# Block 0's attention scores in eight visits instead of nine, with the last head group spread over eight later visits

## The chip, the core and the metric

The kernel runs on one core of a Trainium2 chip. The metric is the device time of one execution in microseconds (us). The engines of the core run side by side, each through its own list of instructions in order: TensorE (PE in the profile, its weight loads PEld), VectorE (DVE), ScalarE (ACT), GpSimd (POOL) and SyncE (SP, which here only starts DMAs). They wait for each other by semaphores.

## The reference

A transformer layer on 2048 tokens of width 1024: attention over a sliding window of 256 with 32 heads of width 32, then a dense part of width 3584. Inputs are bf16.

```python
qkv = layernorm(x) @ wqkv                     # 32 heads of 32
scores = einsum("bhqd,bhkd->bhqk", q, k) * 32 ** -0.5
mask = (i - j >= 0) & (i - j < 256)
p = softmax(where(mask, scores, -1e9))
h = x + einsum("bhqk,bhkd->bhqd", p, v) @ wo
h2 = h + silu(layernorm(h) @ w1) @ w2
```

## The kernel before

The 2048 tokens are four **blocks** of 512 (`b`), and the 32 heads eight **groups** of four (`g`). The pair has one number, `i = 8 * b + g`; `G` is 8.

*The dense stream.* PE computes V, then Q and K by block, then the output projection `wo`, in groups of eight matmuls of 512 columns (`v_group`, `qk_group`, `wo_group`). A group accumulates in one of three PSUM banks in turn (`next_acc`; banks 0 to 2 of `four`), and then a copy, here on DVE, takes it to SBUF (`CAST` at L262 or L272). After this come the two matmuls of the dense part (L786, L814), which the change does not touch.

*Attention in the stream.* `between(kt)` is called ahead of each dense matmul and counts them; a count is called a **slot** below (the first matmul of Q and K of block 0 is slot 0). At fixed slots it runs one of two things:

- a **visit** computes scores. The scores are transposed (keys on partitions, 64 at a time; queries along the columns), and one matmul uses 32 rows by 64 columns of PE, so that the four heads of a group and the two halves of 64 keys run side by side. A visit computes one **unit** of all four heads into `sc` (four banks, one for each head), and up to three extra heads of other units, each 512 columns, into single banks;
- a **piece** (`attn_piece`) multiplies the masked exponentials of two heads of one group with V (18 matmuls in block 0, 24 later) into bank 3, and DVE normalises the result from there (`attn_norm`: a reciprocal at L482, a multiplication at L483) into one of three `obuf` buffers. After the second piece of a group a transposing DMA (L491) takes it from `obuf` to `qT`, whose columns are no longer needed as queries.

*The three extra banks of a visit.* When a visit runs, `now` is the bank that the dense group is filling. `idle` is the next one, which the next group will fill; `behind` is the one that the previous group filled, free once DVE has copied it; `out` is bank 3, free once the last piece's norm has read it:

```python
now = acc_n[0] % 3
idle, behind, out = (now + 1) % 3, (now + 2) % 3, 3
```

Every visit starts after four matmuls of a dense group. After its scores, ACT exponentiates each extra bank and then `sc` (`exp_c`, `exp_0`, `exp_xy`; L328, L428, L334 and L335), and POOL zeroes what the window's edges cut off (`select`, L461).

*Block 0* has 16 units (`2 * g` and `2 * g + 1`). The first nine visits (`visit_0`, slots 108, 132, 148 and so on to 244) compute one unit and three heads of others each, as `VISITS_0` lists: 63 of the 64 heads. The 64th, head 3 of unit 15, is computed in the first visit of period 0.

*Blocks 1 to 3* go in twelve **periods** (`p`) of 48 slots, from slot `t = 256 + 48 * p`, two groups (`i`, `i + 1`) in each. A period has three visits, at `t + 4`, `t + 20` and `t + 36` (`visit(i, n)`, n = 0, 1, 2), and four pieces, at `t + 42`, `t + 47`, `t + 59` and `t + 76`; the last two fall into the next period. The units X and Y of a group and its edge blocks C are shared out over the visits. n = 1 and n = 2 have three extra heads (one C in `idle`, two of X in `out` and `behind`); n = 0 has two (two of C in `idle` and `out`), and in period 0 a third, head 3 of unit 15, in `behind`.

*The order inside a visit* is made in `scores`, L375 to L397. For each head and half it lists the extra bank's matmuls and those of `sc`: banks in `ahead` (`idle`, and `out` in n = 0) go before `sc`, others behind. Each matmul gets a position `at`, the number of columns of its head that come before it, and L388 sorts by that:

```python
todo.sort(key=lambda m: m[0])
```

*Storage.* Block 0's exponentials lie in `r_e`, five columns of 128 for each head, at the offsets of `POS_0`. `r_a` holds queries, keys and V; `qT[3]` and `kT[3]` in it are filled by `qk_group` in block 3 (slots 512 to 703).

Of the kernel before, what the change touches and what calls it, by code (L numbers as in the profile page):

```python
# [11 lines left out]
ACT = mybir.ActivationFunctionType  # L12
ALU = mybir.AluOpType

P = 128
# [22 lines left out]
    [(0, "X", 2), (1, "Y", 1), (2, "X", 3)],  # L38
    [(1, "Y", 2), (2, "C", 1), (3, "Y", 3)],
]  # L40
POS_0 = [(0, 3072, 5632, 7936, 8192, 10752)["ZABNCD".index(c)] for c in "ZCABCDZBACDBZAND"]
VISITS_0 = [
# [3 lines left out]
]  # L46
PIECE_0 = {"X": (0, 128, 512, 320), "Y": (0, 128, 256, 512)}
FIRST = [
# [6 lines left out]
def kernel(  # L55
# [49 lines left out]
    def view(region, off, *dims):  # L105
        n = 1
        for d in dims:
            n *= d
        ap = region[:, off:off + n]
        if len(dims) == 2:  # L110
            return ap.rearrange("p (a b) -> p a b", b=dims[1])
        if len(dims) == 3:
            return ap.rearrange("p (a b c) -> p a b c", b=dims[1], c=dims[2])
        return ap
# [29 lines left out]
    def full_of(e):  # L144
        return e[:, 2048:2560].rearrange("p (h q) -> p h q", q=P)

    obuf = [view(r_n, 512 * i, 4, P) for i in range(3)]
    h_blk = [view(r_a, w2_off + 4096 * 4, 4, D)] + [view(r_e, 8192, 4, D)] * 3
    ln2T = [view(r_a, w2_off + 4096 * 5, KT, 512), view(r_e, 0, KT, 512), view(r_e, 4096, KT, 512), view(r_e, 0, KT, 512)]

# [152 lines left out]
    def chunk_of(i, bank, piece, h):  # L303
        if i >= G and bank == "C":
            return c_ring[:, (i + 1) % 3, h, piece * P:(piece + 1) * P]
        if i >= G:
            c0 = 2048 + mid_at(i, bank, h) * P if piece == 2 else h * 512 + (piece - piece // 3) * P
        else:
            c0 = POS_0[2 * i + (bank != "X")] + h * 640 + (384 if bank == "C" else PIECE_0[bank][piece])
            return r_e[:, c0:c0 + P]  # L310
        return (xbuf if bank == "X" else ybuf)(i)[:, c0:c0 + P]

    def unit_xy(i, odd):
        q0 = odd * P
        mid, first, last = odd, odd - 2, odd + 2
        return [
            [(i, mid, q0, q0 + 320, 64), (i, last, q0 + 256, q0 + 384, 384), (i, first, q0, q0 + 64, 0)],
            [(i, mid, q0 + 64, q0 + 384, 128), (i, first, q0, q0 + 128, 0), (i, last, q0 + 320, q0 + 384, 448)],
        ]

    def unit_c(i):
        pair = (i, i + 1) if (i + 1) % 3 < (i + 2) % 3 else (i + 1, i)
        return [[(ii, kt, q * P, q * P + P, (n * 2 + m) * P)
                 for n, ii in enumerate(pair) for m, (kt, q) in enumerate(((-1, 0), (2, 3)))]] * 2
# [17 lines left out]
    def visit(i, n):  # L342


        now = acc_n[0] % 3
        idle, behind, out = (now + 1) % 3, (now + 2) % 3, 3
        if n == 0:
            own, e_own = unit_xy(i, 0), xbuf(i)
            more = [(1, idle, unit_c(i)), (2, out, unit_c(i))]
            if i == G:  # L350
                more.append((3, behind, unit_0(15)))
        elif n == 1:
            own, e_own = unit_xy(i, 1), ybuf(i)
            more = [(3, idle, unit_c(i)), (0, out, unit_xy(i + 1, 0)), (1, behind, unit_xy(i + 1, 0))]
        else:
            own, e_own = unit_xy(i + 1, 1), ybuf(i + 1)
            more = [(0, idle, unit_c(i)), (2, out, unit_xy(i + 1, 0)), (3, behind, unit_xy(i + 1, 0))]
        scores(own, more, (idle, out)[:2 if n == 0 else 1])
        side = [h for h, _, unit in more if n and len(unit[0]) == 3]
        for h, bank, unit in more:  # L360
            if h in side:
                exp_xy(xbuf(i + 1), four[bank].rearrange("p (h q) -> p h q", h=1), h, h + 1, mid_at(i + 1, "X", h))
            elif len(unit[0]) == 4:
                exp_c(i, h, bank)
            else:
                exp_0(15, h, bank)
                select_0(15, h, h + 1)
                join_0(15, h, h + 1)
        if side:
            select_xy(xbuf(i + 1), side[0] // 2)  # L370
        exp_xy(e_own, sc[:], 0, 4)
        for pair in range(2):
            select_xy(e_own, pair)

    def scores(own, more, ahead):  # L375
        todo = []
        for h in range(4):
            for half in range(2):
                runs = [(sc[:, h, :], own[half])]
                for hh, bank, unit in more:  # L380
                    if hh == h:
                        runs.insert(0 if bank in ahead else 1, (four[bank], unit[half]))
                at = 0
                for bank, parts in runs:
                    for p in parts:
                        todo.append((at, h, half, bank, p))
                        at += p[3] - p[2]
        todo.sort(key=lambda m: m[0])  # L388
        for _, h, half, bank, (ii, kt, qa, qb, col) in todo:
            b, g = divmod(ii, G)  # L390
            t = b * 4 + kt
            r0, k0 = h * DH, (t % 4) * P + half * 64
            nc.tensor.matmul(  # L393
                bank[half * 64:half * 64 + 64, col:col + qb - qa],
                lhsT=kT[t // 4][r0:r0 + DH, g, k0:k0 + 64], rhs=qT[b][r0:r0 + DH, g, qa:qb],
                start=True, stop=True, tile_position=(r0, half * 64),
            )  # L397

    def unit_0(m):
        i, odd = divmod(m, 2)  # L400
        if odd:
            return [
                [(i, 1, 128, 448, 0), (i, 3, 384, 512, 320), (i, 2, 448, 512, 448)],
                [(i, 1, 128, 512, 0), (i, 3, 448, 512, 384), (i, 2, 448, 512, 448)],
            ]
        return [[(i, 0, 0, 320, 0), (i, 2, 256, 448, 320)], [(i, 0, 0, 384, 0), (i, 2, 320, 448, 384)]]

    def heads_0(m, h0, h1):
        return r_e[:, POS_0[m] + 640 * h0:POS_0[m] + 640 * h1].rearrange("p (h q) -> p h q", q=640)

    def select_0(m, h0, h1):
        e = heads_0(m, h0, h1)

        if m % 2:
            select(e[:, :, 0:P], e[:, :, 0:P], True)
            select(e[:, :, 512:640], e[:, :, 320:448], True)
            select(e[:, :, 256:384], e[:, :, 256:384], False)
        else:
            select(e[:, :, 512:640], e[:, :, 256:384], False)
            select(e[:, :, 0:P], e[:, :, 0:P], True)  # L420
            select(e[:, :, 320:448], e[:, :, 320:448], True)
# [2 lines left out]
        nc.gpsimd.tensor_copy(out=heads_0(m, h0, h1)[:, :, 384:448], in_=heads_0(m - 1, h0, h1)[:, :, 448:512])  # L424

    def exp_0(m, h, bank):
        at = POS_0[m] + 640 * h
        nc.scalar.activation(out=r_e[:, at:at + 512], in_=four[bank], func=ACT.Exp, scale=scale)  # L428

    def visit_0(k):  # L430

# [48 lines left out]
    def attn_norm(i, pair):  # L480
        recip = small.tile([P, 8, 1], F32, name="recip", tag="recip")
        nc.vector.reciprocal(out=recip[:], in_=o_ps[:, :, DH:VW])  # L482
        nc.vector.tensor_tensor(  # L483
            out=obuf[i % 3][:, :, pair * 64:(pair + 1) * 64].rearrange("p t (h d) -> p t h d", d=DH),
            in0=o_ps[:, :, 0:DH].rearrange("p (t h) d -> p t h d", h=2),
            in1=recip[:].rearrange("p (t h) o -> p t h o", h=2).to_broadcast([P, 4, 2, DH]), op=ALU.mult,
        )

    def attn_transpose(b, g):
        i = b * G + g  # L490
        nc.sync.dma_start_transpose(out=qT[b][:, g, :].rearrange("p (t q) -> p t q", q=P),  # L491
                                    in_=obuf[i % 3].rearrange("p t d -> p (t d)"))

    def attn_piece(i, pair):
        b, g = divmod(i, G)
# [4 lines left out]
    class Attention:  # L500


        def __init__(self):
            self.seen = 0
            self.visits, self.pieces = {}, {}
            at = [108, *range(132, 260, 16)]
            for k in range(9):
                self.visits[at[k]] = lambda k=k: visit_0(k)
            gaps = (1, 4), (1, 10), (2, 4), (3, 4), (4, 4), (4, 10), (5, 4), (5, 10), (6, 4), (6, 10), (7, 4), (7, 10), (8, 4), (8, 10)
            for d, (k, late) in enumerate(gaps):  # L510
                self.pieces[at[k] + late] = (d // 2, d % 2)
            self.pieces.update({267: (G - 1, 0), 284: (G - 1, 1)})
            for p in range((NB - 1) * G // 2):
                i, t = G + 2 * p, 256 + 48 * p
                for n in range(3):
                    self.visits[t + 4 + 16 * n] = lambda i=i, n=n: visit(i, n)
                for n in range(4):
                    self.pieces[t + (42, 47, 59, 76)[n]] = (i + n // 2, n % 2)

        def between(self, kt):  # L520
            if self.seen in self.pieces:
# [345 lines left out]
```

## Time and profile before

| | us |
|---|---|
| median of 3 runs | 687.12 |
| lowest and highest | 686.51, 687.13 |
| the profiled execution's own time | 686.61 |
| its span, first to last instruction | 684.9 |

The profile is of one execution. A row of the timeline gives the start from the span's first instruction in us, the length of the merged stretch in us, the engine and line, what is written from what, shapes, the number of instructions, and in brackets how long the engine was idle before and what ended that. A row of the group view gives busy time in us and the mean of one instruction in ns, then idle time before them. A stretch's row gives its length and the busy time of each engine in it. Period 0 lies at 88.2 to 103 us of the span, each later one takes about 14.8 us.

### The profile page before, as it was taken

The numbers are of one execution on the slowest core, as the hardware profiler recorded it, in microseconds if no ns is written. First come the engines' busy times: TensorE is split into PE (matmuls) and PEld (weight loads), VectorE is DVE, ScalarE is ACT, GpSimd is POOL, SyncE is SP. The second block draws the span as 40 slices with busy tenths as digits, with TensorE's granted clock in tenths as the row PEclk, the third lists the DMA queues.
The fourth block names the chain that finished last, engine by engine and source line by source line (L and its number), as shares of the span: only waits on it lengthen the run. The fifth ranks groups of instructions, "written<-read, shape, count | busy, mean of one in ns | idle before, by whom it ended". The sixth has DMA issues, their size and how long they took to land.

```text
span 684.9 us, 14583 instructions
## 1 busy us (share of the span) xinstructions
PE 681.0 (99%) x6200; PEld 337.9 (49%) x6200; DVE 292.1 (43%) x615; ACT 237.0 (35%) x402; POOL 161.2 (24%) x287
## 2 busy tenths in 40 slices
PE   9999999999999999999999999999999999999998
PEld 4445555555555555444444444444444444444445
DVE  5277755764444446733416144352233261344111
ACT  7337676767676664023300033200133100233000
POOL 1026987576767665000000000000000000000000
DMA  8823154125531589864033310033200123100110
GB/s 275 262 51 91 31 61 99 26 46 116 163 93 55 172 264 250 204 243 171 1 121 103 64 36 1 0 96 79 71 1 0 43 83 84 39 1 0 32 38 24
DMA packets 77617, 61.50 MB, mean 90 GB/s; under 512 B 52464, under 2 KB 60656, under 8 KB 77552
## 3 DMA queue, kind: packets, MB, share of 16 engines
q1 hardware_dynamic: 77408, 60.31, 32.5%
q8 instruction: 48, 0.79, 0.5%
q10 hardware_dynamic: 144, 0.26, 0.1%
q14 instruction: 17, 0.14, 0.1%
HBM read 39.85 MB, written 8.39 MB: 70 GB/s over the span
## 4 chain that ended last, share of the span: by engine, by line
PE 99%; DMA 1%; SPq 0%; DVE 0%; issue 0%
PE bank L270 17%; PE hacc L786 16%; PE hacc L814 15%; PE bank L814 13%; PE bank L786 12%; PE bank L291 8%; PE bank L260 7%; PE bank L471 5%; PE sc L393 2%; PE bank L393 2%; PE bank L603 1%; DMA r_w<-in_A_wqkv_dram 1%; PE tp L260 1%; PE tp L555 0%; SPq L181 0%; SPq L158 0%
## 5 line engine op out<-in xcount | busy, mean ns | idle before, releaser
L461 POOL TENSOR_SCALAR_AFFINE_SELECT r_e<-r_e 128x512 bf16<-128x512 bf16 (+3 forms) x264 | 154.7, 598 | 106.4 <-ACT r_e L334 48.3
L814 PEld LDWEIGHTS <-r_a 128*128 128x128 bf16 x952 | 90.9, 98 | 103.0
L786 PEld LDWEIGHTS <-r_w 128*128 128x128 bf16 x896 | 87.7, 98 | 105.7
L814 PE MATMUL hacc<-r_a 128*128 128x512 bf16 (+2 forms) x532 | 103.7, 357 | 0.0
L814 PE MATMUL bank<-r_a 128*128 128x512 bf16 x420 | 91.8, 379 | 0.0
L786 PE MATMUL hacc<-r_e,r_w 128*128 128x512 bf16 x384 | 84.8, 379 | 0.0
L270 PEld LDWEIGHTS <-r_w 128*128 128x128 bf16 x512 | 45.2, 97 | 47.7
L786 PE MATMUL bank<-r_e,r_w 128*128 128x512 bf16 x288 | 64.4, 379 | 0.0
L270 PE MATMUL bank<-r_t,r_w 128*128 128x512 bf16 x256 | 62.2, 379 | 0.0
L272 DVE CAST r_a<-bank 128x512 bf16<-128x512 f32 x57 | 39.3, 689 | 47.3 <-PE bank L270 36.2
L270 PE MATMUL bank<-r_w 128*128 128x512 bf16 x256 | 58.9, 379 | 0.0
L291 PE MATMUL bank<-r_o,r_a 128*128 128x512 bf16 x256 | 58.9, 379 | 0.0
L334 ACT ACTIVATE r_e<-sc 128x1536 bf16<-128x1536 f32 x36 | 53.5, 1485 | 0.0
L471 PEld LDWEIGHTS <-r_e 128*128 128x128 bf16 x1440 | 45.6, 96 | 15.1
L795 ACT ACTIVATE r_n<-bank 128x512 f32<-128x512 f32 x18 | 10.7, 597 | 117.0 <-PE bank L786 117.0
L328 ACT ACTIVATE r_e<-bank 128x512 bf16<-128x512 f32 x48 | 27.4, 596 | 57.3 <-PE bank L393 43.3
L471 PE MATMUL bank<-r_a,r_e 128*128 128x33 bf16 x1440 | 46.2, 178 | 0.0
L795 ACT ACTIVATE r_n<-hacc 128x512 f32<-128x512 f32 x24 | 14.3, 597 | 75.5 <-PE hacc L786 75.5
L829 DVE SCALAR_TENSOR_TENSOR r_t<-bank,r_t 128x512 bf16<-128x512 f32 x15 | 10.3, 684 | 66.6 <-PE bank L814 66.6
L291 PEld LDWEIGHTS <-r_a 128*128 128x128 bf16 x256 | 23.3, 97 | 25.7
L829 DVE SCALAR_TENSOR_TENSOR r_t<-hacc,r_t 128x512 bf16<-128x512 f32 (+2 forms) x19 | 12.0, 632 | 53.5 <-PE hacc L814 53.5
L393 PEld LDWEIGHTS <-r_a 32*64 32x64 bf16 x1856 | 23.7, 103 | 19.3 <-issue 19.1
(100 smaller groups left out, 602.2 us busy)
## 6 DMA issues: line engine op xcount, KB each, us to landing
r_w<-in_B_w_dram SPq DMA_DIRECT2D x8, 896.0 KB, 5.5
r_a<-in_B_w_dram SPq DMA_DIRECT2D x7, 1024.0 KB, 9.3
r_w<-in_A_wqkv_dram SPq DMA_DIRECT2D x4, 1024.0 KB, 8.4
r_t<-h_dram SPq DMA_DIRECT2D x16, 256.0 KB, 3.0
out_dram<-r_t SPq DMA_DIRECT2D x31, 128.0 KB, 1.7
r_e<-h_dram SPq DMA_DIRECT2D x3, 1024.0 KB, 5.9
r_o<-in_A_x_dram SPq DMA_DIRECT2D x11, 256.0 KB, 5.5
r_a<-in_A_x_dram SPq DMA_DIRECT2D x10, 256.0 KB, 5.0
```

Source lines behind the costliest of these rows:

```text
L260: nc.tensor.matmul(acc, lhsT=lnT_b[b % 2][:, kt, j * P:(j + 1) * P], rhs=wv[:, kt, c * 512:(c + 1) * 512], start=(kt == 0), stop=(kt == KT ...
L270: nc.tensor.matmul(acc, lhsT=wqk[:, kt, col0:col0 + P], rhs=lnT_b[b % 2][:, kt, :], start=(kt == 0), stop=(kt == KT - 1))
L272: copy(out=(qT, kT)[which][b][:, g, :], in_=acc)
L291: nc.tensor.matmul(acc, lhsT=qT[b][:, g, j * P:(j + 1) * P], rhs=wo[:, g, c * 512:(c + 1) * 512], start=(g == 0), stop=(g == G - 1))
L328: nc.scalar.activation(out=c_ring[:, lo:hi + 1:hi - lo, h, :], in_=four[bank].rearrange("p (n q) -> p n q", q=256), func=ACT.Exp, scale=scale)
L334: nc.scalar.activation(out=tri_of(e)[:, h0:h1, :, 64:256], in_=tri, func=ACT.Exp, scale=scale)
L393: nc.tensor.matmul(bank[half * 64:half * 64 + 64, col:col + qb - qa], lhsT=kT[t // 4][r0:r0 + DH, g, k0:k0 + 64], rhs=qT[b][r0:r0 + DH, g, ...
L461: nc.gpsimd.affine_select(out=dst, in_=src, pattern=[[0, n] for n in dst.shape[1:-1]] + [[sgn, P]], compare_op=ALU.is_ge if upper else ALU ...
L471: nc.tensor.matmul(o_ps[:, qt * 2 + hh, 0:VW], lhsT=chunk_of(i, bank, piece, pair * 2 + hh), rhs=v[:, b * 4 + kt, g * 4 + pair * 2 + hh, : ...
L786: nc.tensor.matmul(acc, lhsT=w1[:, kt, ft * P:(ft + 1) * P], rhs=ln2T[b][:, kt, :], start=(kt == 0), stop=(kt == KT - 1))
L795: nc.scalar.activation(out=th, in_=acc, func=ACT.Tanh, scale=0.5)
L814: nc.tensor.matmul(acc[:, 0:c1 - c0], lhsT=gT[:, ft, j * P:(j + 1) * P], rhs=w2[ft // 4][:, ft % 4, c0:c1], start=(ft == 0), stop=(ft == F ...
```

## The change

Block 0's ninth visit (slot 244: unit 14 and three heads of unit 15) is dropped, with its rows of `POS_0` and `VISITS_0`. The eight heads of units 14 and 15, those of group 7, are computed one at a time in the first visits (n = 0) of periods 0 to 7, each as a third extra head in the bank `behind`: period p takes head `p // 2` of unit `14 + p % 2`. In the periods where that head is 1 or 2, the two C heads of n = 0 are others than 1 and 2, and those of n = 1 and n = 2 follow from it.

In these eight visits the order of the scores changes too (`longest`): `at` is now minus the number of columns that the head still has to do, so that heads with most left go first, the one without an extra head last, and among equals the longest matmul first.

POOL's masks of the moved head come after those of the visit's own unit. The exponentials of units 14 and 15 lie in `r_a`, in columns of `qT[3]` (unit 14) and `kT[3]` (unit 15), and group 7's normalised output in `kT[3]`'s columns of g = 7.

Group 7's two pieces move from slots 267 and 284 (period 0) to slots `t + 32` of periods 3 and 7 (432 and 624), and its transposing DMA moves from behind slot 284 to behind slot 624. In the periods 2 and 6 the last piece goes one slot earlier, from `t + 76` to `t + 75`.

```diff
-POS_0 = [... for c in "ZCABCDZBACDBZAND"]
+POS_0 = [... for c in "ZCABCDZBACDBZA"]
 VISITS_0 = [
...
-    (11, (10, 2), (10, 3), (12, 0)), (13, (12, 1), (12, 2), (12, 3)), (14, (15, 0), (15, 1), (15, 2)),
+    (11, (10, 2), (10, 3), (12, 0)), (13, (12, 1), (12, 2), (12, 3)),
 ]
...
+    o_last = view(r_a, 28672 + 3584, 4, P)
+    def obuf(i):
+        return o_last if i == G - 1 else obufs[i % 3]
...
+        p = (i - G) // 2
+        rest = (14 + p % 2, p // 2) if n == 0 and p < 8 else None
+        c0, c1 = {1: (0, 2), 2: (1, 3)}.get(p // 2, (1, 2))
         if n == 0:
             own, e_own = unit_xy(i, 0), xbuf(i)
-            more = [(1, idle, unit_c(i)), (2, out, unit_c(i))]
-            if i == G:
-                more.append((3, behind, unit_0(15)))
+            more = [(c0, idle, unit_c(i)), (c1, out, unit_c(i))]
+            if rest:
+                more.append((rest[1], behind, unit_0(rest[0])))
...
-        scores(own, more, (idle, out)[:2 if n == 0 else 1])
+        scores(own, more, (idle, out)[:2 if n == 0 else 1], bool(rest))
...
+        if rest:
+            m, h = rest
+            select_0(m, h, h + 1)
+            if m % 2:
+                join_0(m, h, h + 1)
...
-                at = 0
+                at = -sum(p[3] - p[2] for _, parts in runs for p in parts) if longest else 0
...
-        todo.sort(key=lambda m: m[0])
+        todo.sort(key=lambda m: (m[0], m[4][2] - m[4][3] if longest else 0))
...
     def heads_0(m, h0, h1):
-        return r_e[:, POS_0[m] + 640 * h0:POS_0[m] + 640 * h1].rearrange("p (h q) -> p h q", q=640)
+        if m < len(POS_0):
+            region, at = r_e, POS_0[m]
+        else:
+            region, at = r_a, 28672 * (m % 2) + 768 * (h0 // 2)
+        return region[:, at + 640 * h0:at + 640 * h1].rearrange("p (h q) -> p h q", q=640)
...
-            for k in range(9):
+            for k in range(8):
                 self.visits[at[k]] = lambda k=k: visit_0(k)
...
-            self.pieces.update({267: (G - 1, 0), 284: (G - 1, 1)})
...
-                    self.pieces[t + (42, 47, 59, 76)[n]] = (i + n // 2, n % 2)
+                    self.pieces[t + (42, 47, 59, 75 if p in (2, 6) else 76)[n]] = (i + n // 2, n % 2)
+            for k in range(2):
+                self.pieces[256 + 48 * (4 * k + 3) + 32] = (G - 1, k)
```

More of the change, by code (lines that the diff above doesn't have):

```diff
@@ L40 @@
 ]
-POS_0 = [(0, 3072, 5632, 7936, 8192, 10752)["ZABNCD".index(c)] for c in "ZCABCDZBACDBZAND"]
+POS_0 = [(0, 3072, 5632, 7936, 8192, 10752)["ZABNCD".index(c)] for c in "ZCABCDZBACDBZA"]
 VISITS_0 = [
@@ L145, in full_of @@
         return e[:, 2048:2560].rearrange("p (h q) -> p h q", q=P)
-    obuf = [view(r_n, 512 * i, 4, P) for i in range(3)]
+    obufs = [view(r_n, 512 * i, 4, P) for i in range(3)]
+    o_last = view(r_a, 28672 + 3584, 4, P)
+    def obuf(i):
+        return o_last if i == G - 1 else obufs[i % 3]
     h_blk = [view(r_a, w2_off + 4096 * 4, 4, D)] + [view(r_e, 8192, 4, D)] * 3
@@ L308, in chunk_of @@
         else:
-            c0 = POS_0[2 * i + (bank != "X")] + h * 640 + (384 if bank == "C" else PIECE_0[bank][piece])
-            return r_e[:, c0:c0 + P]
+            c0 = 384 if bank == "C" else PIECE_0[bank][piece]
+            return heads_0(2 * i + (bank != "X"), h, h + 1)[:, 0, c0:c0 + P]
         return (xbuf if bank == "X" else ybuf)(i)[:, c0:c0 + P]
@@ L346, in visit @@
         idle, behind, out = (now + 1) % 3, (now + 2) % 3, 3
+        p = (i - G) // 2
+        rest = (14 + p % 2, p // 2) if n == 0 and p < 8 else None
+        c0, c1 = {1: (0, 2), 2: (1, 3)}.get(p // 2, (1, 2))
         if n == 0:
             own, e_own = unit_xy(i, 0), xbuf(i)
-            more = [(1, idle, unit_c(i)), (2, out, unit_c(i))]
-            if i == G:
-                more.append((3, behind, unit_0(15)))
+            more = [(c0, idle, unit_c(i)), (c1, out, unit_c(i))]
+            if rest:
+                more.append((rest[1], behind, unit_0(rest[0])))
         elif n == 1:
             own, e_own = unit_xy(i, 1), ybuf(i)
-            more = [(3, idle, unit_c(i)), (0, out, unit_xy(i + 1, 0)), (1, behind, unit_xy(i + 1, 0))]
+            more = [(5 - c1, idle, unit_c(i)), (0, out, unit_xy(i + 1, 0)), (1, behind, unit_xy(i + 1, 0))]
         else:
             own, e_own = unit_xy(i + 1, 1), ybuf(i + 1)
-            more = [(0, idle, unit_c(i)), (2, out, unit_xy(i + 1, 0)), (3, behind, unit_xy(i + 1, 0))]
-        scores(own, more, (idle, out)[:2 if n == 0 else 1])
+            more = [(1 - c0, idle, unit_c(i)), (2, out, unit_xy(i + 1, 0)), (3, behind, unit_xy(i + 1, 0))]
+        scores(own, more, (idle, out)[:2 if n == 0 else 1], bool(rest))
         side = [h for h, _, unit in more if n and len(unit[0]) == 3]
@@ L365, in visit @@
             else:
-                exp_0(15, h, bank)
-                select_0(15, h, h + 1)
-                join_0(15, h, h + 1)
+                exp_0(rest[0], h, bank)
         if side:
@@ L373, in visit, with scores @@
             select_xy(e_own, pair)
-    def scores(own, more, ahead):
+        if rest:
[3 more added lines that the diff above has]
+                join_0(m, h, h + 1)
+    def scores(own, more, ahead, longest=False):
         todo = []
@@ L426, in exp_0 @@
     def exp_0(m, h, bank):
-        at = POS_0[m] + 640 * h
-        nc.scalar.activation(out=r_e[:, at:at + 512], in_=four[bank], func=ACT.Exp, scale=scale)
+        nc.scalar.activation(out=heads_0(m, h, h + 1)[:, 0, 0:512], in_=four[bank], func=ACT.Exp, scale=scale)
     def visit_0(k):
@@ L483, in attn_norm @@
         nc.vector.tensor_tensor(
-            out=obuf[i % 3][:, :, pair * 64:(pair + 1) * 64].rearrange("p t (h d) -> p t h d", d=DH),
+            out=obuf(i)[:, :, pair * 64:(pair + 1) * 64].rearrange("p t (h d) -> p t h d", d=DH),
             in0=o_ps[:, :, 0:DH].rearrange("p (t h) d -> p t h d", h=2),
@@ L491, in attn_transpose @@
         nc.sync.dma_start_transpose(out=qT[b][:, g, :].rearrange("p (t q) -> p t q", q=P),
-                                    in_=obuf[i % 3].rearrange("p t d -> p (t d)"))
+                                    in_=obuf(i).rearrange("p t d -> p (t d)"))
     def attn_piece(i, pair):
```

## The prediction

> **What bounds the kernel now.** I read the page first: what is the bound, and is any of it waiting?
>
> ```profile
> span 684.9 us, 14583 instructions
> PE 681.0 (99%) x6200; PEld 337.9 (49%) x6200; DVE 292.1 (43%) x615; ACT 237.0 (35%) x402; POOL 161.2 (24%) x287
> PE 99%; DMA 1%; SPq 0%; DVE 0%; issue 0%
> ```
>
> PE fills the span and the chain, so only what changes PE's time counts: matmuls that go, and waits that come. The timeline of PE shows what a visit costs, between the dense matmuls on either side. First the removed visit (34 scores, from 84.35), then the first visit of period 0 (46, from 89.39) and its second (44, from 94.08), then the first of period 1 (40, from 104.05). Columns are start, length, engine, line, instruction, count.
>
> ```profile
> 82.97 1.46 PE L270 MATMUL bank<-r_t,r_w 128*128 128x512 bf16 x6
> 84.35 0.53 PEld L393 LDWEIGHTS <-r_a 32*64 32x64 bf16 x34 [0.42 <-issue]
> 84.93 1.04 PE L270 MATMUL bank<-r_t,r_w 128*128 128x512 bf16 x4
> ...
> 88.00 1.46 PE L270 MATMUL bank<-r_t,r_w 128*128 128x512 bf16 x6
> 89.38 0.65 PEld L393 LDWEIGHTS <-r_a 32*64 32x64 bf16 x46 [0.42 <-issue]
> 89.73 0.35 PE L393 MATMUL bank<-r_a 32*64 32x320 bf16 x2
> 90.08 1.68 PE L270 MATMUL bank<-r_t,r_w 128*128 128x512 bf16 x7
> 91.60 0.61 PE L471 MATMUL bank<-r_a,r_e 128*128 128x33 bf16 x18
> 92.05 2.10 PE L270 MATMUL bank<-r_t,r_w 128*128 128x512 bf16 x9
> 94.08 0.54 PEld L393 LDWEIGHTS <-r_a 32*64 32x64 bf16 x44 [0.42 <-issue]
> 94.33 0.31 PE L393 MATMUL bank<-r_a 32*64 32x320 bf16 x4
> 94.67 1.90 PE L270 MATMUL bank<-r_t,r_w 128*128 128x512 bf16 x8
> 96.41 0.61 PE L471 MATMUL bank<-r_a,r_e 128*128 128x33 bf16 x18
> 96.87 1.89 PE L270 MATMUL bank<-r_t,r_w 128*128 128x512 bf16 x8
> 98.68 0.55 PEld L393 LDWEIGHTS <-r_a 32*64 32x64 bf16 x44 [0.42 <-issue]
> ...
> 102.88 1.24 PE L270 MATMUL bank<-r_t,r_w 128*128 128x512 bf16 x5
> 104.05 0.51 PEld L393 LDWEIGHTS <-r_a 32*64 32x64 bf16 x40 [0.42 <-issue]
> 104.62 0.60 PE L270 MATMUL bank<-r_t,r_w 128*128 128x512 bf16 x2
> ```
>
> Six dense matmuls take 1.46 us, and the group view gives 0.379 for one alone:
>
> ```profile
> L270 PE MATMUL bank<-r_t,r_w 128*128 128x512 bf16 x256 | 62.2, 379 | 0.0
> ```
>
> So they follow each other every (1.46 - 0.379) / 5 = 0.216 us, and undisturbed the next starts 0.163 before such a row ends. What a visit adds is the rest of the gap: the removed one 84.93 - (84.43 - 0.163) = **0.66 us**; period 0's first 90.08 - 89.30 = 0.78; its second 94.67 - 93.99 = 0.68; period 1's first 104.62 - 103.96 = 0.66. A third extra head costs 0.02 where all is in step (0.68 against 0.66, 44 scores against 40), and 0.12 in period 0's first visit, where the third bank's first score came 89.73 - 89.38 = 0.35 after the visit's start; in the second visit it came 94.33 - 94.08 = 0.25 after.
>
> **The change part by part.** *The visit that goes*: -0.66. Its 28 head-scores are 7 of 64; the eight heads of units 14 and 15 now ride in first visits, one of them there already.
>
> *The order in the eight first visits.* Period 0's keeps three extra heads, but sorts the heads with most left to do first, so the third bank's long scores stand early in the queue. I take it to the second visit's price: 0.78 to 0.68, -0.10. Bounds: 0 (what delayed it was not the order) to -0.12.
>
> *The third bank in periods 1 to 7* is the heart of the change. That bank is the one which the previous dense group has just filled, and DVE must copy it out first. These are DVE's rows ahead of period 0's, period 1's and period 7's first visits, with period 7's visit:
>
> ```profile
> 88.78 0.68 DVE L272 CAST r_a<-bank 128x512 bf16<-128x512 f32 x1
> ...
> 103.31 0.42 DVE L483 TENSOR_TENSOR r_n<-bank,recip 128x256 bf16<-128x256 f32 x1
> 103.65 0.68 DVE L272 CAST r_a<-bank 128x512 bf16<-128x512 f32 x1
> ...
> 192.70 0.68 DVE L272 CAST r_a<-bank 128x512 bf16<-128x512 f32 x1
> 193.10 0.51 PEld L393 LDWEIGHTS <-r_a 32*64 32x64 bf16 x40 [0.42 <-issue]
> ```
>
> In period 0 the copy ends at 89.46, 0.08 after the visit's start: no wait. In period 1 it ends at 104.33, **0.28** after the start, in period 7 at 193.38, again 0.28: an output piece sits one matmul before the group's end, and its L483 norm runs ahead of the copy on DVE. From DVE's end to PE there is one tight row pair:
>
> ```profile
> 11.74 0.55 DVE L581 TENSOR_SCALAR r_o<-r_o,mean,rs_a 128x1024 bf16<-128x1024 bf16 x1
> 12.34 0.34 PEld L555 LDWEIGHTS <-r_o 128*128 128x128 bf16 x4 [0.20 <-DVE r_o L581]
> ```
>
> 12.29 to 12.34: 0.05. So the third bank opens at 0.28 + 0.05 = 0.33, and its head has done its own 512 columns by 0.25. PE takes its matmuls in order, so behind the waiting score stand the long second halves of the other heads too, and then the dense group: the visit ends 0.08 later. Price per visit: 0.02 + 0.08 = **0.10**, seven times: **+0.70**. Bounds: 0.02 (no wait; 0.14 in all) to 0.20 (a wait of 0.08, and on top the 0.10 that separates 0.78 from 0.68; 1.40 in all). The value lies near the upper of the two like rows: a third bank that opened at 0.35 cost 0.12.
>
> By the Trainium skill, TensorE: Matmul & The Clock Gate, Part 3, matmuls start and end strictly in program order and only weight loads are pulled ahead; by that rule the waiting score holds the whole visit, as I count it, and if only its own tile waited the sum would be the same, since that tile then ends last.
>
> *Output pieces.* Group 7's two leave period 0 and come back in periods 3 and 7 with the same 18 matmuls: 92.05 - (91.76 - 0.163) = 0.45 and 96.87 - (96.57 - 0.163) = 0.46, taken away and added: 0. Their cover for ACT goes too:
>
> ```profile
> 90.05 1.09 ACT L328 ACTIVATE r_e<-bank 128x512 bf16<-128x512 f32 x2 [1.70 <-PE bank L393]
> 91.02 0.61 ACT L428 ACTIVATE r_e<-bank 128x512 bf16<-128x512 f32 x1
> 92.83 0.63 ACT L335 ACTIVATE r_e<-sc 128x512 bf16<-128x512 f32 x1
> 97.47 0.66 ACT L335 ACTIVATE r_e<-sc 128x512 bf16<-128x512 f32 x1
> ```
>
> ACT frees the four score banks at 93.46, 0.62 before the visit at 94.08; without the piece (0.45) and with a first visit shorter by 0.10, 0.07 is left. Next, 98.13 against 98.68: 0.55 - 0.46 = 0.09. Both are above 0.05, so I count 0; if the margins are misjudged, 0.1 at each, +0.2. In periods 3 and 7 the piece at slot 32 stands at a group's first matmul, four ahead of a visit that needs its bank; one stands like that now, and this is the dense row behind it and the end of its norm:
>
> ```profile
> 86.25 1.46 PE L270 MATMUL bank<-r_t,r_w 128*128 128x512 bf16 x6
> 86.84 0.42 DVE L483 TENSOR_TENSOR r_n<-bank,recip 128x256 bf16<-128x256 f32 x1
> ```
>
> The norm ends at 87.26, with 0.05 at 87.31; the visit would want the bank at 86.25 + 4 x 0.216 + 0.25 = 87.36: 0, at worst 0.1 each.
>
> *ACT, POOL, DMA.* The exponentials and masks of the moved heads:
>
> ```profile
> L450 ACT ACTIVATE r_e<-sc 128x2048 bf16<-128x2048 f32 x9 | 17.1, 1898 | 0.0
> L428 ACT ACTIVATE r_e<-bank 128x512 bf16<-128x512 f32 x28 | 14.8, 598 | 14.3 <-PE bank L393 13.0 <-POOL r_e L461 1.3
> L461 POOL TENSOR_SCALAR_AFFINE_SELECT r_e<-r_e 128x128 bf16<-128x128 bf16 x9 | 2.5, 292 | 1.8 <-ACT r_e L428 1.6
> 89.38:104.04 14.66, 14.66 (x267) 8.29 (x266) 7.60 (x17) 10.48 (x19) 11.70 (x22) 1.00 0.64 74
> 104.04:118.87 14.83, 14.83 (x273) 8.43 (x272) 7.99 (x18) 9.99 (x18) 9.96 (x17) 1.00 0.49 109
> ```
>
> ACT gives up 1.898 + 4 x 0.598 and gets 8 x 0.598: +0.5 us, spread as 0.6 per period. POOL gets three selects of 0.292 in each first visit and a join in every second. The last two rows are periods 0 and 1 by engine (PE, PEld, DVE, ACT, POOL): ACT would go from 9.99 to 10.6 and POOL from 9.96 to about 11, and period 0 ran with 10.48 and 11.70 in a shorter period and PE full. Cost 0; without that cover each late exponential holds PE for at most its 0.6. One transpose DMA of group 7 moves on SP's queue from period 0 to period 7, behind a w1 load that waits for nothing in that place; what reads it comes in the last projection, so 0. The moved heads' exponentials and group 7's output lie in columns of `qT[3]` and `kT[3]` that block 3 fills later; the tightest new wait, of DVE's copy at slot 648 on the piece at 624, has 24 dense matmuls (5.2 us) of room, with the next group's copy queued behind it: 0.
>
> **Sum**: -0.66 - 0.10 + 0.70 = -0.06 us. The profiled run took 686.61 for a span of 684.9; the median shown is 687.12, 0.51 above it. So 686.55 by the profiled run, 687.06 by the median: **687.1**.
>
> **The rivals.** *The wait is hidden*: the bank opens in time after all, because PE reaches the third bank later than 0.25, or the copy ends earlier since fewer matmuls ran before it. For it: 0.08 is small. Against it: the 0.28 repeats to 0.01 in both rows. -0.66 - 0.10 + 0.14 = -0.62: 686.5.
>
> *The wait drains the queue* (slower than before): the visit stands still with the rest of its scores undelivered, and after the copy they come late, at 0.20 a visit, seven visits, period 0's staying at 0.78: -0.66 + 1.40 = +0.74: 687.9. It decides once a visit loses over 0.11 ((0.66 + 0.10) / 7). For it: the 46-score visit did lose 0.10 with its bank free since 0.08 (89.46). Against: there the late score was the 33rd of the visit (28 of a lower position `at` and four of the same stand before it in the order of L388), and in the new order the waiting one is the 23rd. By the Trainium skill, the same page, the table's queue row, TensorE's queue holds 64 instructions, which is 32 pairs of load and matmul; that fits the late 33rd, and by it the 23rd would be at hand.
>
> *ACT becomes the bound in the first period*: +0.2 from the two thin margins, 687.3. By the Trainium skill, TensorEngine Tiling (Array Packing), PSUM Bottleneck, packing speeds TensorE but not the emptying of PSUM, which may become the limit; the trace bears this out for DVE's copy at 0.28, not yet for ACT, idle for a third of each period.
>
> **How the numbers follow.** Forecast 0.55, of its own 686.8 to 687.4 (half the runs' spread of 686.51 to 687.13 to each side); hidden wait 0.15; drained queue 0.15; ACT 0.05; a cause that none of these names 0.10. The range takes in the rivals with the runs' spread: 686.2 to 688.0. A measurement of this kernel tells about 0.2%, 1.4 us, from no change, and all four cases lie inside: even with no wait at all, less than one visit is won. Only the unnamed cause goes past it: faster 0.04, same 0.86, slower 0.10.
>
> **What would show it.** One visit fewer on PE; first visits of periods 1 to 7 at about 0.76, with the third bank's first score 0.33 after their start and just behind the end of DVE's copy; period 0's first at 0.68; no PE idle ahead of period 0's second and third visits. If the first visits cost 0.68, the hidden wait was right; at 0.86, the drained queue. A change of over 1.4 us would mean a wait that I have not seen, outside the eight visits.

## The result and the profile after

The changed kernel takes **687.88 us** (median of 18 runs, 687.34 to 688.86), the kernel before 686.67 in the 18 runs beside them (686.23 to 687.15): a ratio of 1.0018, 95% interval 1.001 to 1.0025. The forecast was 687.1 against 687.12, no change; the kernel became slower by 1.2 us. That is just inside the 0.2% that the forecast called the same, but the interval lies wholly above 1. The changed kernel's lines stand 5 to 15 further down: scores L404, pieces L485, Q and K L275, their copy L277, the norm of a piece L496 and L497, the layernorm's normalisation L234 (L229 before).

The page of the changed kernel: its span, the engines, and the chain that ended last.

```profile
span 686.1 us, 14503 instructions
PE 672.4 (98%) x6097; PEld 338.1 (49%) x6200; DVE 291.7 (43%) x615; ACT 237.2 (35%) x405; POOL 163.0 (24%) x304
PE 97%; issue 1%; DMA 1%; DVE 0%; SPq 0%
```

The span grew by 1.2. PE's 98% misleads: of 6200 matmuls 103 records are missing from this trace, and a gap in the records reads as idle time. The weight loads are all there, so I measure with them: from a visit's first load to the next dense one, and from visit to visit. The loads of the kernel before (start, length, count): the first visit, the dense row after period 0's first, period 3's third and what follows it, and the last visit.

```profile
44.09 0.53 PEld L393 LDWEIGHTS <-r_a 32*64 32x64 bf16 x34 [0.42 <-issue]
...
90.07 1.19 PEld L270 LDWEIGHTS <-r_w 128*128 128x128 bf16 x7
...
143.22 0.55 PEld L393 LDWEIGHTS <-r_a 32*64 32x64 bf16 x44 [0.42 <-issue]
143.81 0.98 PEld L270 LDWEIGHTS <-r_w 128*128 128x128 bf16 x6
...
261.94 0.55 PEld L393 LDWEIGHTS <-r_a 32*64 32x64 bf16 x44 [0.42 <-issue]
```

The same places of the changed kernel, with period 0's three visits and the first ones of periods 1 and 7:

```profile
44.05 0.53 PEld L404 LDWEIGHTS <-r_a 32*64 32x64 bf16 x34 [0.42 <-issue]
...
88.68 0.54 PEld L404 LDWEIGHTS <-r_a 32*64 32x64 bf16 x44 [0.42 <-issue]
89.26 3.14 PEld L275 LDWEIGHTS <-r_w 128*128 128x128 bf16 x16
92.82 0.54 PEld L404 LDWEIGHTS <-r_a 32*64 32x64 bf16 x44 [0.42 <-issue]
...
96.96 0.55 PEld L404 LDWEIGHTS <-r_a 32*64 32x64 bf16 x44 [0.42 <-issue]
...
102.31 0.63 PEld L404 LDWEIGHTS <-r_a 32*64 32x64 bf16 x46 [0.42 <-issue]
103.01 1.19 PEld L275 LDWEIGHTS <-r_w 128*128 128x128 bf16 x7
...
142.31 0.34 PEld L404 LDWEIGHTS <-r_a 32*64 32x64 bf16 x29 [0.42 <-issue]
143.76 0.28 PEld L404 LDWEIGHTS <-r_a 32*64 32x64 bf16 x15 [1.10 <-issue]
144.10 0.98 PEld L275 LDWEIGHTS <-r_w 128*128 128x128 bf16 x6
...
193.75 0.63 PEld L404 LDWEIGHTS <-r_a 32*64 32x64 bf16 x46 [0.42 <-issue]
194.45 0.55 PEld L275 LDWEIGHTS <-r_w 128*128 128x128 bf16 x4
...
263.18 0.55 PEld L404 LDWEIGHTS <-r_a 32*64 32x64 bf16 x44 [0.42 <-issue]
```

From the first visit to the last it was 261.94 - 44.09 = 217.85 and is 263.18 - 44.05 = 219.13: **+1.28**, the whole loss. It splits into four terms:

| term | from the rows | us | forecast |
|---|---|---|---|
| the removed visit | first visit to period 0's first: 45.29 (89.38 - 44.09), now 44.63 | -0.66 | -0.66 |
| period 0's first visit | 90.07 - 89.38 = 0.69, now 89.26 - 88.68 = 0.58 | -0.11 | -0.10 |
| seven first visits, periods 1 to 7 | 104.62 - 104.05 = 0.57, now 103.01 - 102.31 = 0.70 and 194.45 - 193.75 = 0.70; 0.12 each in the single records | +0.85 | +0.70 |
| period 3's third visit | 143.81 - 143.22 = 0.59, now 144.10 - 142.31 = 1.79 | +1.19 | 0 |

They add up to +1.27, and rounding makes the rest. Every other visit has its old length to 0.01, and period 0's second and third visits come with no wait, as forecast. The fourth term is the surprise: after 29 of the visit's 44 loads comes a hole of 1.10. PE's waits name it, in a row that this view does not have in the kernel before (who waited for whom, us in total, times, longest):

```profile
PE bank L404 <- DVE r_a L497: 0.9, 1, 0.9
```

The piece on PE, DVE's rows ahead of the release, and the score that was released:

```profile
140.91 0.61 PE L485 MATMUL bank<-r_a 128*128 128x33 bf16 x18
...
141.11 0.69 DVE L277 CAST r_a<-bank 128x512 bf16<-128x512 f32 x1 [0.35 <-PE bank L275]
141.72 1.41 DVE L234 TENSOR_SCALAR r_o<-r_o,st_a,rs_a 128x1024 bf16<-128x1024 bf16 x2
...
143.28 0.42 DVE L497 TENSOR_TENSOR r_a<-bank,recip 128x256 bf16<-128x256 f32 x1
143.75 0.33 PE L404 MATMUL bank<-r_a 32*64 32x320 bf16 x4 [0.89 <-DVE r_a L497]
```

Group 7's piece at slot 432 was done on PE by 141.52. Its norm had to wait for two normalisations of block 3's layernorm, 1.41 us, which stand ahead of it in DVE's list; it freed bank 3 at 143.70, and the visit's `out` scores began at 143.75. In the kernel before, the same two ran at that slot with no piece behind them:

```profile
143.07 1.40 DVE L229 TENSOR_SCALAR r_o<-r_o,st_a,rs_a 128x1024 bf16<-128x1024 bf16 x2
```

So the trace of before showed them, beside the visit at 143.22 that now waits.

### The profile page after: what moved, and what is told of

Same layout as the page of the kernel before. It is cut to its first block, busy times and chain, and to the rows that moved or that the text cites. A ratio compares the mean times of both kernels' runs of the same rounds, so it can differ in the third digit from the quotient of the medians.

```text
span 686.1 us, 14503 instructions
## 1 busy us (share of the span) xinstructions
PE 672.4 (98%) x6097; PEld 338.1 (49%) x6200; DVE 291.7 (43%) x615; ACT 237.2 (35%) x405; POOL 163.0 (24%) x304
## 4 chain that ended last, share of the span: by engine, by line
PE 97%; issue 1%; DMA 1%; DVE 0%; SPq 0%
PE hacc L801 16%; PE bank L275 16%; PE hacc L829 15%; PE bank L829 13%; PE bank L801 12%; PE bank L296 8%; PE bank L265 6%; PE bank L485 5%; PE sc L404 2%; PE bank L404 2%; PE bank L618 1%; DMA r_w<-in_A_wqkv_dram 1%; PE tp L265 1%; DVE r_o L234 0%; DVE r_a L277 0%
## 5 line engine op out<-in xcount | busy, mean ns | idle before, releaser
L475 POOL TENSOR_SCALAR_AFFINE_SELECT r_e<-r_e 128x512 bf16<-128x512 bf16 (+3 forms) x255 | 150.5, 604 | 105.6 <-ACT r_e L339 48.6
L275 PEld LDWEIGHTS <-r_w 128*128 128x128 bf16 x512 | 45.4, 97 | 47.8
L277 DVE CAST r_a<-bank 128x512 bf16<-128x512 f32 x57 | 39.2, 688 | 50.7 <-PE bank L275 38.9
L275 PE MATMUL bank<-r_t,r_w 128*128 128x512 bf16 x233 | 58.1, 379 | 2.3 <-issue 1.6
L275 PE MATMUL bank<-r_w 128*128 128x512 bf16 x240 | 56.7, 379 | 1.5 <-issue 1.0
L296 PE MATMUL bank<-r_o,r_a 128*128 128x512 bf16 x242 | 56.8, 379 | 1.3 <-issue 0.8
L485 PEld LDWEIGHTS <-r_e 128*128 128x128 bf16 x1404 | 44.4, 96 | 14.6
L485 PE MATMUL bank<-r_a,r_e 128*128 128x33 bf16 x1404 | 45.0, 178 | 0.1
L404 PEld LDWEIGHTS <-r_a 32*64 32x64 bf16 x1856 | 23.9, 103 | 20.1 <-issue 19.8
```

The source lines that it names most:

```text
L275: nc.tensor.matmul(acc, lhsT=wqk[:, kt, col0:col0 + P], rhs=lnT_b[b % 2][:, kt, :], start=(kt == 0), stop=(kt == KT - 1))
L277: copy(out=(qT, kT)[which][b][:, g, :], in_=acc)
L296: nc.tensor.matmul(acc, lhsT=qT[b][:, g, j * P:(j + 1) * P], rhs=wo[:, g, c * 512:(c + 1) * 512], start=(g == 0), stop=(g == G - 1))
L404: nc.tensor.matmul(bank[half * 64:half * 64 + 64, col:col + qb - qa], lhsT=kT[t // 4][r0:r0 + DH, g, k0:k0 + 64], rhs=qT[b][r0:r0 + DH, g, ...
L475: nc.gpsimd.affine_select(out=dst, in_=src, pattern=[[0, n] for n in dst.shape[1:-1]] + [[sgn, P]], compare_op=ALU.is_ge if upper else ALU ...
L485: nc.tensor.matmul(o_ps[:, qt * 2 + hh, 0:VW], lhsT=chunk_of(i, bank, piece, pair * 2 + hh), rhs=v[:, b * 4 + kt, g * 4 + pair * 2 + hh, : ...
```

## The experiments

**Theory.** Two waits for DVE's in-order list eat the removed visit: the stall in period 3 (two normalisations ahead of a norm) and 0.12 in each of seven first visits (the copy of the bank behind). **Rivals**: the stall comes from the moved piece itself or its new place in `r_a`; the 0.12 is the price of a third head and has nothing to do with the copy.

### The layernorm steps two dense groups earlier (e1_ln_early)

```diff
-                for _ in range(1 if len(steps) > 8 else 2):
+                for _ in range({7: 2, 9: 3, 11: 2, 13: 0, 15: 2}.get(n, 1)):
```

This is block 2's loop at L756, with n the dense group. Steps stand behind every second group; slot 432 opens group 14. The two normalisations that stood behind group 13 now stand behind group 11, which is two groups earlier (the expectation counts it as one), and nothing is left behind group 13.

> The changed kernel with the layernorm steps of block 2 pulled one dense group forward, so that no 1024-column normalisation stands on DVE just ahead of the output piece at slot 432. Theory (DVE's in-order queue: two normalisations of 1.41 us in all hold that piece's norm, and with it bank 3 for the visit at slot 436): period 3's third visit shrinks from 1.78 us, first weight load to the next dense one, to 0.59, and the time falls by 1.19 us against the changed kernel, to about 686.7, level with the kernel before. Rival (the piece itself is late: its masks, its exponentials in the new place, or the output buffer in the new place): the visit stays at 1.78 and the time at 687.9.

Period 3's third visit, and DVE ahead of it:

```profile
142.43 0.56 PEld L404 LDWEIGHTS <-r_a 32*64 32x64 bf16 x44 [0.42 <-issue]
143.03 0.98 PEld L275 LDWEIGHTS <-r_w 128*128 128x128 bf16 x6
```

```profile
141.23 0.69 DVE L277 CAST r_a<-bank 128x512 bf16<-128x512 f32 x1 [0.35 <-PE bank L275]
...
142.07 0.42 DVE L497 TENSOR_TENSOR r_a<-bank,recip 128x256 bf16<-128x256 f32 x1
```

The visit is 0.60 long, its loads in one piece; the norm follows the copy at once. The time is 686.64 us, ratio to before 1.0004 (0.9995 to 1.0013), against a forecast of 686.7. With the piece, its place and the new buffer unchanged the stall is gone, so the rival falls.

### The piece one period later (e2_piece_p4)

```diff
-... 75 if p in (2, 6) else 76 ...
+... 75 if p in (3, 6) else 76 ...
-                self.pieces[256 + 48 * (4 * k + 3) + 32] = (G - 1, k)
+                self.pieces[256 + 48 * (3 * k + 4) + 32] = (G - 1, k)
```

> The changed kernel with the first output piece of group 7 at slot 480 (period 4) instead of 432 (period 3); the early fourth piece goes with it. No layernorm step stands on DVE there. Theory (the queue on DVE): no visit is longer than 0.70 us, the time falls by 1.19 us to about 686.7. Rival (an extra piece in front of a visit costs this wherever it stands, or the new output buffer does): the stall of 1.2 us moves to period 4's third visit and the time stays at 687.9.

The third visits of periods 3 and 4:

```profile
142.25 0.56 PEld L404 LDWEIGHTS <-r_a 32*64 32x64 bf16 x44 [0.42 <-issue]
142.85 0.55 PEld L275 LDWEIGHTS <-r_w 128*128 128x128 bf16 x4
...
157.67 0.53 PEld L404 LDWEIGHTS <-r_a 32*64 32x64 bf16 x44 [0.42 <-issue]
158.25 0.33 PEld L275 LDWEIGHTS <-r_w 128*128 128x128 bf16 x3
```

They take 0.60 and 0.58: no stall in the old place or the new. The time is 686.39 us, ratio 1.0002 (0.9993 to 1.0011). A piece ahead of a visit costs nothing of itself here; what stands on DVE at that slot decides. The changed kernel says the same in period 7: its piece at slot 624 has no normalisation ahead of it, since no block follows block 3, and the visit behind it takes 0.58 as before.

### One normalisation instead of two (e7_ln_one)

```diff
-... {7: 2, 9: 3, 11: 2, 13: 0, 15: 2} ...
+... {7: 2, 9: 3, 11: 1, 13: 1, 15: 2} ...
```

The diff is against the first experiment's kernel.

> The changed kernel with one normalisation instead of two on DVE ahead of the output piece at slot 432; the other layernorm steps as in the run that pulled them forward. Theory (the queue): one normalisation of 0.54 to 0.85 us less, so the stall of 1.19 us in period 3's third visit falls to 0.35 to 0.65. Rival (a fixed delay, by whatever starts it): it stays near 1.19 or is gone.

The visit's loads, then DVE:

```profile
142.31 0.34 PEld L404 LDWEIGHTS <-r_a 32*64 32x64 bf16 x29 [0.42 <-issue]
142.98 0.28 PEld L404 LDWEIGHTS <-r_a 32*64 32x64 bf16 x15 [0.33 <-issue]
143.32 0.76 PEld L275 LDWEIGHTS <-r_w 128*128 128x128 bf16 x5
```

```profile
141.71 0.64 DVE L234 TENSOR_SCALAR r_o<-r_o,st_a,rs_a 128x1024 bf16<-128x1024 bf16 x1
...
142.50 0.42 DVE L497 TENSOR_TENSOR r_a<-bank,recip 128x256 bf16<-128x256 f32 x1
```

The visit takes 143.32 - 142.31 = 1.01, 0.42 over its 0.59, inside the forecast 0.35 to 0.65 (one run, 687.07 us beside 687.03 for the kernel before; the visit tells, not the time). The stall goes with the length of what stands ahead, as a queue does: 1.41, 0.64 and 0 us of normalisations give stalls of 1.19, 0.42 and 0.01, the first two each 0.22 less: by so much may the norm be late before the visit needs its bank.

### The first visits one matmul later (e3_visit_late)

```diff
-                    self.visits[t + 4 + 16 * n] = lambda i=i, n=n: visit(i, n)
+                    self.visits[t + 4 + 16 * n + (n == 0 and 0 < p < 8)] = lambda i=i, n=n: visit(i, n)
```

> The changed kernel with the first visits of periods 1 to 7 one dense matmul later, so that DVE's copy of the bank behind has 0.216 us more. Theory (each of the seven waits for that copy): they shrink from 0.69-0.70 us to 0.58, seven times 0.12, and the time falls by 0.85 us to about 687.0; the stall in period 3's third visit stays. Rival (a third extra head costs 0.12 by itself, through the number of scores or the queue): they stay at 0.69-0.70 and the time at 687.9.

Period 1's first visit, and period 3's third:

```profile
102.76 0.55 PEld L404 LDWEIGHTS <-r_a 32*64 32x64 bf16 x46 [0.42 <-issue]
103.35 0.55 PEld L275 LDWEIGHTS <-r_w 128*128 128x128 bf16 x4
...
142.21 0.34 PEld L404 LDWEIGHTS <-r_a 32*64 32x64 bf16 x29 [0.42 <-issue]
143.88 0.28 PEld L404 LDWEIGHTS <-r_a 32*64 32x64 bf16 x15 [1.33 <-issue]
144.22 0.76 PEld L275 LDWEIGHTS <-r_w 128*128 128x128 bf16 x5
```

The first visit falls from 0.70 to 0.59, with the same three extra heads and the same 46 scores; in the single records the visits of periods 2, 4 and 6, with 44 scores, fall to 0.58. With two extra heads they all took 0.57 before. So a third head costs 0.00 to 0.02 by itself, and the rest of the 0.12 was the wait for the copy and what the wait delayed. The time missed its forecast of 687.0, at 687.31 (ratio 1.0014, 1.0005 to 1.0023), for two reasons: the seven visits fell by 0.77 together and not by 0.85, and the stall in period 3 grew by 0.23, from 1.19 to 2.01 - 0.59 = 1.42; the last section says on what.

### Both edits (e4_both)

> The changed kernel with both edits: block 2's layernorm steps one group forward, and the first visits of periods 1 to 7 one matmul later. Theory: both waits gone, 687.9 - 1.19 - 0.85 = 685.8, which is the removed visit (0.66) and period 0's order (0.11) with nothing given back: 0.1% below the kernel before. Rival (the later visits push the wait elsewhere, to the next dense group's bank, whose exponential then has one matmul less): 0.2 to 0.8 us of it comes back, 686.0 to 686.6.

The diffs of the first and the fourth experiment together. The first visit of all, period 1's first, period 3's third, and the last of all:

```profile
44.38 0.53 PEld L404 LDWEIGHTS <-r_a 32*64 32x64 bf16 x34 [0.42 <-issue]
...
102.86 0.55 PEld L404 LDWEIGHTS <-r_a 32*64 32x64 bf16 x46 [0.42 <-issue]
103.45 0.55 PEld L275 LDWEIGHTS <-r_w 128*128 128x128 bf16 x4
...
142.31 0.56 PEld L404 LDWEIGHTS <-r_a 32*64 32x64 bf16 x44 [0.42 <-issue]
142.91 0.98 PEld L275 LDWEIGHTS <-r_w 128*128 128x128 bf16 x6
...
261.55 0.55 PEld L404 LDWEIGHTS <-r_a 32*64 32x64 bf16 x44 [0.42 <-issue]
```

They take 0.59 and 0.60: neither wait is left. From first to last visit it is 261.55 - 44.38 = 217.17, 0.68 less than before: the removed visit and the order, 0.77 together, less 0.09 for the seven third heads, which the expectation left out. The time is **685.78 us**, ratio to before 0.999 (0.9981 to 0.9999): 0.1% faster than the kernel before, the interval just clear of 1. This is what the change would have won with its waits taken away. The rival, a wait pushed to the next group's bank, did not come: beside these terms the stretch from first to last visit is the old one to 0.01.

### The order alone (e5_order_alone)

The kernel before, with the change's two lines of the order for period 0's first visit alone:

```diff
-        scores(own, more, (idle, out)[:2 if n == 0 else 1])
+        scores(own, more, (idle, out)[:2 if n == 0 else 1], n == 0 and i == G)
...
-                at = 0
+                at = -sum(p[3] - p[2] for _, parts in runs for p in parts) if longest else 0
...
-        todo.sort(key=lambda m: m[0])
+        todo.sort(key=lambda m: (m[0], m[4][2] - m[4][3] if longest else 0))
```

> The kernel before with the new order of scores in period 0's first visit alone; nine visits of block 0, all else as before. Theory (the order was what made that visit long): from 0.69 us, first weight load to the next dense one, to 0.58 to 0.60, and no other visit changes: 0.1 us in all. Rival (it became short in the changed kernel because its third head is one of unit 14 with 44 scores instead of one of unit 15 with 46): it stays at 0.69.

```profile
89.70 0.55 PEld L393 LDWEIGHTS <-r_a 32*64 32x64 bf16 x46 [0.42 <-issue]
90.29 0.76 PEld L270 LDWEIGHTS <-r_w 128*128 128x128 bf16 x5
```

The visit takes 0.59 instead of 0.69 with the same 46 scores: the order made it long. One run, 686.83 us beside 687.03, can't show 0.1 us; the visit's length can.

### The waiting scores last among equals (e6_wait_last)

```diff
-        todo.sort(key=lambda m: (m[0], m[4][2] - m[4][3] if longest else 0))
+        todo.sort(key=lambda m: (m[0], longest and m[3] is four[more[-1][1]], m[4][2] - m[4][3] if longest else 0))
```

> The changed kernel with one tie broken otherwise: among scores of equal rank those of the bank behind come last, so that six long scores stand ahead of the waiting one and not behind it. Theory (0.096 of the 0.122 is the wait itself, the rest comes from the eight tiles starting together after it): the seven visits shrink from 0.695 us to about 0.67. Rival (the waiting head is last in any case and sets the end alone): they stay at 0.69 to 0.70. A third (the head that waits would have been done by then): 0.58.

```profile
101.86 0.61 PEld L404 LDWEIGHTS <-r_a 32*64 32x64 bf16 x46 [0.42 <-issue]
102.53 0.55 PEld L275 LDWEIGHTS <-r_w 128*128 128x128 bf16 x4
```

The visit takes 0.67 instead of 0.70, and all seven 0.67 to 0.68 in the single records. So 0.02 of the 0.12 came from the long scores that stood behind the waiting one; the 0.10 left is the wait, with the 0.00 to 0.02 of the third head itself. One run: 687.25 us.

## Why the prediction was wrong, point by point

- **The removed visit, -0.66**: right, -0.66.
- **Period 0's order, -0.10**: right, -0.11; the order alone gave 0.10, with 46 scores where the changed kernel has 44.
- **The third bank in periods 1 to 7, +0.70**: the mechanism right, the size a little small. The copy and the first score released by it, in period 1's first visit of the changed kernel:

```profile
101.92 0.68 DVE L277 CAST r_a<-bank 128x512 bf16<-128x512 f32 x1
```

```profile
102.66 0.32 PE L404 MATMUL bank<-r_a 32*64 32x384 bf16 x2
```

The copy ends at 102.60 and the score starts at 102.66, 0.35 after the visit's start at 102.31 (forecast 0.33). The visit lost 0.12, not 0.10: the score came 0.02 later than forecast, and the long scores behind it, which the prediction names but gives no price, cost 0.02. That is more than the 0.02 that was missing: a third head without a wait cost 0.00 to 0.02, and the score that came 0.10 late made the visit end only 0.08 to 0.10 later. That the like row of period 0 had also lost 0.12 (0.78 for 0.66) is chance: its bank was free, and the order alone took 0.10 of it away.
- **The drained queue, 0.20 a visit**: wrong; all seven visits lost 0.12. That the time came out at this rival's 687.9 is luck. It meant +0.74 on 687.12, with period 0's first visit staying long; measured was +1.21 on 686.67, and 1.19 of that stands in a visit that the rival does not touch. For the same reason the range of 686.2 to 688.0 holds the measured time without holding its cause.
- **The hidden wait**: wrong, as those visits show.
- **ACT as the bound in period 0**: wrong. The visit after the first came at 92.82 - 88.68 = 4.14, the next at 96.96 - 92.82 = 4.14 after it, and by the rows of before with the pieces and the order's 0.10 taken off it would be 94.08 - 89.38 - 0.45 - 0.10 = 4.15 and 98.68 - 94.08 - 0.46 = 4.14: no wait came in.
- **The failed step** is in *Output pieces*: "In periods 3 and 7 the piece at slot 32 stands at a group's first matmul, four ahead of a visit that needs its bank; one stands like that now [...]: 0, at worst 0.1 each." In period 7 it was 0; in period 3 it was **1.19**. I took the piece's price from another place, where DVE had only the copy ahead of the norm, and did not read DVE's rows at the place to which the piece moves. They were in the trace of before, two normalisations of 1.40 us in all at 143.07. The forecast gave 0.10 to a cause that it could not name, and expected it "outside the eight visits" only for a change of over 1.4 us; it came there, with 1.2.

Without that step the sum would have been -0.66 - 0.11 + 0.85 = +0.08, no change; the first experiment, the changed kernel without that wait, measured 1.0004 of before.

## What to carry to other kernels

A step that moves takes its place in every engine's list, not only in the one that you look at: read the rows of each engine at the *new* slot in the trace of before, what stands ahead there, and what waits behind. An instruction that frees a buffer for the bound engine should not have long work ahead of it on an in-order engine; moving that work by two dense groups was worth 1.2 us here, nearly twice the removed visit. A bank that PE has filled is free only when its copy has ended: compare that moment with the first use to 0.1 us, since a wait of 0.1 in seven places weighed more here than the visit saved.

## What the runs showed of the hardware beside this

*The normalisation's length.* DVE's 1024-column bf16 normalisation took 0.54 to 0.55 us where POOL had no select running, and 0.54 to 0.98 where one ran (the 0.98 in the first experiment). First the one at 12.39 in the kernel before, alone; then the two ahead of the norm in the run with the first visits one matmul later:

```profile
12.39 0.55 DVE L229 TENSOR_SCALAR r_o<-r_o,st_a,rs_a 128x1024 bf16<-128x1024 bf16 x1
```

```profile
141.62 1.64 DVE L234 TENSOR_SCALAR r_o<-r_o,st_a,rs_a 128x1024 bf16<-128x1024 bf16 x2
```

These two took 1.40 before, 1.41 in the changed kernel and 1.64 in that run; the difference is the 0.23 by which its stall grew. In both runs a select lay over the first of them. In the single records each of the two ends 0.28 after a select does: in the changed kernel the selects end at 142.08 and 142.85 and the normalisations at 142.36 and 143.13, in the later-visit run the selects at 142.21 and 142.97 and the normalisations at 142.49 and 143.25. The first normalisation had started 0.28 after its select in the changed kernel and only 0.05 after it in that run. By the Trainium skill, SBUF — State Buffer, Who interferes with whom, such an instruction can take a port pair that DVE shares with GpSimd, and then one blocks the other; the ends agree with that. It was read from the traces and not tried by itself.

*A waiting score holds the weight loads too.* In period 1's first visit of the changed kernel the single records have the 23rd load 0.22 after the start and the 24th only at 0.34, with the released score. In the run with the first visits one matmul later, where nothing waited, the 24th came at 0.17. By the Trainium skill, TensorE: Matmul & The Clock Gate, Part 3, loads are pulled ahead of matmuls in flight; here none was pulled ahead of one that waits for a semaphore. The 0.02 that came of putting six scores ahead of the waiting one fits this.
